# Attention with rotary embedding and two MoE layers: the first two head pairs scored on 128 rows, fillers moved, last activations of attention reordered

## The chip, the cores and the metric

The kernel runs on one core of a Trainium2 chip. The metric is the device time of one execution in microseconds, median of the runs; before the change it is 603.07 us (three runs, 602.18 to 604.75). The engines are named as in the profile: PE (TensorE, matmuls; PEld is its weight load), DVE (VectorE), ACT (ScalarE), POOL (GpSimd), SP (the queue that issues the DMAs).

## The reference

```python
q_rot, k_rot = rotate(q), rotate(k)            # rotary embedding, (2, 8, 576, 64) each
scores = matmul(q_rot, k_rot^T) / sqrt(64)
attn = softmax(scores)                         # max, exp, sum, divide
x = (attn @ v) -> (1152 tokens, 512)
h = x @ w1_in;  x = elu(h) @ w1_out            # 512 -> 2048 -> 512
h = x @ w2_in;  out = (h * tanh(softplus(h))) @ w2_out
```

The inputs of attention are float32; the weights come as float64 and are converted on the way (DVE and POOL, L96 to L108). To keep float32 accuracy on PE, the kernel splits each operand into a high part (rounded to the fast matmul type) and a low remainder, and adds up the products high by high, low by high and high by low.

## The kernel before

**Pairs and units.** Two heads of 64 dimensions share the 128 partitions: eight head pairs p. A pair has nine units of scores (`tiles`): four blocks of 128 queries for head 0, four for head 1 (L358 gives their order), and a ninth unit that holds the last 64 queries of both heads. Unit u is scored by `do_S`, u = 9p + i. The main loop (L581) takes two units per step w: step w scores units 2w and 2w+1, takes their maxima on DVE (`do_max`, L403) and exponentials on ACT (`do_exp`, L416), and transposes the probabilities P of the two units of step w-1 on PE (`do_T`, L463); the first transpose is copied out by DVE (L479), the second by ACT (L481). There is one PSUM tile for transposes, so the second waits for the first one's copy. `do_av` (L487) multiplies by v a few chunks per step, `do_R` brings the inverse sums into the same layout, `do_x`, `do_xh`, `do_xl` scale the result and split it into XH and XL. A score tile has two PSUM buffers, so a unit is scored when the exponential of the unit two before it is done. Each engine works off its instructions in the order written.

**Two ways of scoring.** For pairs 2 to 7 (`DIRECT`, L376) DMAs stack the parts on 128 partitions ("ka" holds the high part of k over its low part, "qa" twice the high part of q, "qb" the low part over zeros), and a block takes two passes of 128 rows. For pairs 0 and 1 there is no time for this: a block takes three passes on the 64 partitions of its head, `d["qh"][rows, cols]` against `d["kh"][rows, ks]` and so on. The ninth unit uses 128 rows in every pair ("bh", "bl", filled by four small DMAs in `stack_q`).

**Who prepares what.** `rope_part` rotates in three operations, on DVE for k of pair 0, else on POOL. Pair 0 is split piecewise as its data land (`HEAD`, `first_hi` on ACT, `first_lo` on DVE). From pair 1 on, `prepare(p, k)` is called at set places: k=0 splits k (`split_half`: high and low part on POOL, for pair 1 the high part on ACT) and k=1 splits q (both on POOL), each with its DMAs; k=2 to 7 rotate pair p+1 on POOL. The tile "qh" of pairs 1 to 7 has one buffer: POOL can write it for pair 2 only when PE has scored the last block of pair 1.

**Fillers.** `keep_warm(n)` puts n matmuls of zeros by zeros on PE (each shows as two instructions, L533): 20 at the start, and `FILL = (0, 9, 0)`: none after the scores of step 0, nine after those of step 1.

**End of attention.** The first three products of the first MoE layer (`g1_mm`, L207, n = 0, 1, 2) are placed in steps 36, 37 and 38 (`tail(k, False)`). Their activation `elu` is three ACT operations and two on DVE, the second of which (L242) frees the score tile; `elu_hi` on ACT and `elu_lo` on DVE split the result. `tail(k, True)` does this for product 0 at the end of step 37, behind `do_xh` and `do_x` of that step, and for product 1 at the end of step 38. Product n needs the PSUM buffer of product n-2.

The functions that the change touches, with the profile's line numbers:

Of the kernel before, what the change touches and what calls it, by code (L numbers as in the profile page):

```python
# [22 lines left out]
def plain(ap):  # L23
    return ap.bitcast(F32)
# [3 lines left out]
def kernel(  # L28
# [25 lines left out]
    TPP = 9  # L54
# [199 lines left out]
    def attention(att, ps, tail):  # L254
# [3 lines left out]
        psA = [ps.tile([128, 512], F32, name=f"psA{g}") for g in range(2)]  # L258
        HEAD = [(2, slice(0, HS)), (0, slice(0, 128)), (2, slice(HS, S)), (0, slice(128, HS)), (0, slice(HS, S))]
        WARM = 20  # L260
        FILL = (0, 9, 0)
        DIRECT = 2 * TPP
        QSCALE = -1.0 / float(D) ** 0.5
        qk_t = {}
        v_t = {}
# [35 lines left out]

        def split_alloc(p):
            d = {}
            for nm in ("kh", "kl", "ql"):
                d[nm] = att.tile([128, S], F32R, tag=nm, name=nm, bufs=2)
            for nm in (("qa",), (), ("ka", "qa"))[min(p, 2)]:
                d[nm] = att.tile([128, 2, S], F32R, tag=nm, name=nm, bufs=2)
            d["qh"] = att.tile([128, S], F32R, tag="qh", name="qh", bufs=1) if p else d["qa"][:, 0, :]
            i = p % 2
            d["qb"] = qb[i]  # L310
            d["bh"], d["bl"] = bd[i]
            sp_t[p] = d

        def split_half(p, i, h, l):
            d = sp_t[p]
# [4 lines left out]
                nc.gpsimd.tensor_scalar(out=d[h], in0=x, scalar1=1.0, scalar2=0.0, op0=ALU.mult, op1=ALU.add)  # L320
            nc.gpsimd.tensor_tensor(out=d[l], in0=x, in1=plain(d[h]), op=ALU.subtract)

        def first_hi(i, cs):
            nc.scalar.activation(
                out=sp_t[0]["kh" if i else "qh"][:, cs], in_=qk_t[0][:, i, cs],
                func=AF.Copy, scale=1.0 if i else QSCALE,
            )

        def first_lo(i, cs):
            d = sp_t[0]  # L330
            h, l = ("kh", "kl") if i else ("qh", "ql")
            nc.vector.scalar_tensor_tensor(
                out=d[l][:, cs], in0=qk_t[0][:, i, cs], scalar=1.0 if i else QSCALE,
                in1=plain(d[h][:, cs]), op0=ALU.mult, op1=ALU.subtract,
            )

        def spread(dst, src, r):
            for h in range(2):
                nc.sync.dma_start(out=plain(dst[64 * r:64 * r + 64, h, :]), in_=plain(src[64 * h:64 * h + 64, :]))

        def stack_k(p):
            d = sp_t[p]
            if p > 1:
                spread(d["ka"], d["kh"], 0)
                spread(d["ka"], d["kl"], 1)

        def stack_q(p):
            d = sp_t[p]
            for r in range(2 if p > 1 else 0):
                spread(d["qa"], d["qh"], r)  # L350
            if p > 1:
                spread(d["qb"], d["ql"], 0)
            for r in range(2):
                sl = slice(64 * r, 64 * r + 64)
                nc.sync.dma_start(out=plain(d["bh"][sl, 64 * r:64 * r + 64]), in_=plain(d["qh"][sl, S - 64:S]))
                nc.sync.dma_start(out=plain(d["bl"][sl, 64 * r:64 * r + 64]), in_=plain(d["ql"][sl, S - 64:S]))

        tiles = [(0, 0), (0, 1), (1, 0), (1, 1), (0, 2), (0, 3), (1, 2), (1, 3), None]  # L358
        psS = {}
# [7 lines left out]
        def do_S(u):  # L367
            p, i = divmod(u, TPP)
            d = sp_t[p]
            o = ps_s()  # L370
            psS[u] = o
            if tiles[i] is not None:
                h, t = tiles[i]
                rows = slice(64 * h, 64 * h + 64)
                cols = slice(128 * t, 128 * t + 128)
                if u >= DIRECT:  # L376
                    passes = [
                        (d["qa"][:, h, cols], lambda ks: d["ka"][:, h, ks]),
                        (d["qb"][:, h, cols], lambda ks: d["ka"][:, h, ks]),
                    ]  # L380
                else:
                    passes = [
                        (d["qh"][rows, cols], lambda ks: d["kh"][rows, ks]),
                        (d["ql"][rows, cols], lambda ks: d["kh"][rows, ks]),
                        (d["qh"][rows, cols], lambda ks: d["kl"][rows, ks]),
                    ]
            else:
                passes = [
                    (d["bh"], lambda ks: d["kh"][:, ks]),
                    (d["bh"], lambda ks: d["kl"][:, ks]),  # L390
                    (d["bl"], lambda ks: d["kh"][:, ks]),
                ]
            n = len(passes)
            for a, (l, r) in enumerate(passes):
                for j in range(2):
                    nc.tensor.matmul(  # L396
                        o[:, j, :HS], lhsT=l, rhs=r(slice(j * HS, j * HS + HS)),
                        start=(a == 0), stop=(a == n - 1),
                    )

        def do_max(u):
            m = att.tile([128, 1], F32, tag="mn", name="mn", bufs=4)
# [122 lines left out]
            bd.append(pair)  # L525
        qb = [att.tile([128, 2, S], F32R, name=f"qb{i}") for i in range(2)]
        nc.vector.memset(psT[:, 1, 0:128], 0.0)
        for t in qb:
            nc.vector.memset(plain(t[64:128]), 0.0)
        split_alloc(0)  # L530
        def keep_warm(n):
            for _ in range(n):
                nc.tensor.matmul(psA[1][:, 0:128], lhsT=zero, rhs=zero, start=True, stop=True)  # L533
# [3 lines left out]
        for i, cs in HEAD:  # L537
            rope_half(0, i, nc.vector if i else nc.gpsimd, cs)
            if cs.stop < S or i:
                first_hi(i, cs)  # L540
        for i, cs in HEAD[:-1]:
            first_lo(i, cs)
        nc.scalar.activation(out=tab[:, 0:2, :], in_=tab[:, 2:4, :], func=AF.Copy, scale=QSCALE)
        rope_half(1, 2, nc.gpsimd)

        def prepare(p, k):
            if k == 0:
                if p > 1 and p + 1 < NP:
                    load_pair(p + 1)
                split_alloc(p)  # L550
                split_half(p, 2, "kh", "kl")
                stack_k(p)
            elif k == 1:
                split_half(p, 0, "qh", "ql")
                stack_q(p)
            elif p + 1 < NP:
                rope_part(p + 1, 2 if k < 5 else 0, (k - 2) % 3, nc.gpsimd)
# [23 lines left out]
        for w in range(max(av_at) + 2):  # L581
# [36 lines left out]
                do_T(b - 2)  # L618
            if R is not None:
                do_R(*R)  # L620
            if last_end is not None:
                do_xh(*last_end)
                if w > max(av_at):
                    do_xl(*last_end)
# [5 lines left out]
                load_pair(2)  # L630
            if 0 < w <= NW:
                do_evac(b - 2, nc.scalar)
            if w in (1, 2):
                if w == 2:
                    rope_half(1, 0, nc.gpsimd)
                prepare(1, w - 1)
            elif w in (3, 4):
                for k in range(3):
                    prepare(1, 3 * w - 7 + k)
            if end is not None:  # L640
                do_x(*end)
            if w >= NW:
                tmp_pool[0] = att
                tail(w - NW, True)
                tmp_pool[0] = None
            weight_slot(w, (1, 2, 3, 4))
        assert not R_t
        assert njob[0] == len(STAGES) and not staged
# [188 lines left out]

    def tail(k, late):
        if late:
            if k in (1, 2):  # L840
                elu_lo(*elu_hi(*elu(0, k - 1, 0, early[k - 1])))
                early[k - 1] = None
        elif k < 3:
            early[k] = g1_mm(0, k, 0)

# [62 lines left out]
```

## Time and profile before

| | |
|---|---|
| median of three runs | 603.07 us |
| profiled execution | 608.24 us, of which the span is 606.5 us |
| mean granted clock of PE over the span | 0.971 |
| PE busy | 572.2 us (94%) |
| DVE busy | 426.3 us (70%) |
| ACT busy | 360.3 us (59%) |
| POOL busy | 240.7 us (40%) |
| mean of a maximum (DVE L403), of an exponential (ACT L416) | 0.752 us, 0.737 us |
| releasers of PE's idle time from 0 to 62 us | DVE's copy of transposes 3.1 us, DVE's memset of bl 1.5 us, ACT's kh 1.3 us, the DMA of qa 1.0 us |

The granted clock is a share of full speed: 1.00 is 2.4 GHz, 0.50 is 1.2 GHz. "Busy" on PE does not mean full speed: at 0.50 the same matmul takes up to twice as long and counts as busy all along. Attention fills the span up to about 184 us, the first MoE layer to about 412 us, the second the rest. In the page's 40 slices PE is at 9 tenths or more in every slice from the fourteenth (197 us) on, but for the 28th (409 to 425 us) and the last.

### The profile page before, as it was taken

Reading aid. Unit: us, or ns where it says so; the run is one execution under the profiler, and the core shown is the slowest. Engines: PE = TensorE matmul, PEld = TensorE weight load, DVE = VectorE, ACT = ScalarE, POOL = GpSimd, SP = SyncE. Lnnn points to the kernel's source line nnn. Section 1 sums busy time; section 2 is a strip of 40 time slices with the busy share of each in tenths; the row PEclk is TensorE's granted clock in tenths of the full one; section 3 lists DMA queues with packets and bytes.
Section 4 is the critical chain, followed back from the end, with each engine's and each line's share of the span. In section 5 each row is a group of like instructions: output and inputs, shape, how many; then the busy total and the mean of one; then the engine's idle time right before and its main releaser. Section 6 shows DMA issues by size and latency. Waiting matters only on the chain.

```text
span 606.5 us, 10180 instructions
## 1 busy us (share of the span) xinstructions
PE 572.2 (94%) x3850; PEld 511.4 (84%) x3850; DVE 426.3 (70%) x642; ACT 360.3 (59%) x642; POOL 240.7 (40%) x212
## 2 busy tenths in 40 slices
PE   7899989988996999999999999996999999999997
PEld 6766667666785999999999999995799898999985
DVE  6366888988844776677777777898488677674552
ACT  3446657666664656555455465783866858478660
POOL 5483989972021132323323222445244433432000
PEclk8689999999998999999999999999799999999999
DMA  6263786856011122323223223233242432300022
GB/s 216 71 204 102 205 224 204 225 129 159 24 47 35 47 94 78 97 70 98 77 74 102 69 70 105 71 113 112 71 110 76 128 88 73 118 19 1 17 88 86
DMA packets 43121, 60.69 MB, mean 100 GB/s; under 512 B 13760, under 2 KB 31936, under 8 KB 42304
## 3 DMA queue, kind: packets, MB, share of 16 engines
q1 hardware_dynamic: 43072, 60.05, 33.1%
q8 instruction: 30, 0.49, 0.3%
q14 instruction: 19, 0.16, 0.1%
HBM read 46.20 MB, written 2.36 MB: 80 GB/s over the span
## 4 chain that ended last, share of the span: by engine, by line
PE 39%; issue 32%; DVE 13%; POOL 13%; DMA 1%; SPq 1%; ACT 1%; POOLq 0%; DVEq 0%; ACTq 0%
PE ps_h L742 17%; PE ps_s L207 13%; PE ps_s L396 4%; POOL wu L96 4%; DVE mn L403 4%; PE psT L463 4%; DVE pt L479 3%; POOL wi1l L128 3%; POOL wo0l L128 2%; POOL wo1l L128 2%; POOL wi0l L128 2%; PE psA L487 1%; DVE wu L104 1%; DVE R L432 1%; DVE wu L108 1%
## 5 line engine op out<-in xcount | busy, mean ns | idle before, releaser
L416 ACT ACTIVATE P<-ps_s,mn 128x576 f32<-128x576 f32 x72 | 52.8, 737 | 34.3 <-DVE mn L403 34.0
L403 DVE TENSOR_REDUCE mn<-ps_s 128x1 f32<-128x576 f32 x72 | 51.9, 752 | 29.1 <-PE ps_s L396 29.0
L463 PE MATMUL psT<-idn,P 128*128 128x128 f32 (+1 forms) x360 | 55.6, 287 | 12.9 <-DVE pt L479 12.8
L463 PEld LDWEIGHTS psT<-idn,P 128*128 128x128 f32 (+1 forms) x360 | 39.4, 139 | 31.1 <-DVE pt L479 25.8
L207 PE MATMUL ps_s<-XH,wi0h 128*128 128x288 f32 x256 | 55.7, 300 | 5.5 <-DVE P L242 5.4
L128 POOL TENSOR_TENSOR wo0l<-wu,wo0h 128x512 fp32r<-128x512 f32 x16 | 25.3, 1582 | 87.3 <-ACT wo0h L125 87.3
L100 DVE TENSOR_SCALAR wu<-wu 128x512 int32<-128x512 int32 x64 | 34.2, 534 | 35.1 <-POOL wu L96 35.1
L207 PE MATMUL ps_s<-XH,wi1h 128*128 128x288 f32 x256 | 55.1, 296 | 1.4 <-ACT tb L670 1.4
L128 POOL TENSOR_TENSOR wi1l<-wu,wi1h 128x512 fp32r<-128x512 f32 x16 | 25.3, 1578 | 78.2 <-ACT wi1h L125 78.2
L207 PE MATMUL ps_s<-XL,wi0h 128*128 128x288 f32 x256 | 55.2, 297 | 0.0
L207 PE MATMUL ps_s<-XH,wi0l 128*128 128x288 f32 x256 | 55.1, 297 | 0.0
L207 PE MATMUL ps_s<-XH,wi1l 128*128 128x288 f32 x256 | 54.8, 295 | 0.0
L207 PE MATMUL ps_s<-XL,wi1h 128*128 128x288 f32 x256 | 54.8, 295 | 0.0
L104 DVE SCALAR_TENSOR_TENSOR wu<-raw,wu 128x512 int32<-128x512 int32 x64 | 50.1, 782 | 1.8
L108 DVE SCALAR_TENSOR_TENSOR wu<-raw,wu 128x512 int32<-128x512 int32 x64 | 48.9, 765 | 1.6
L128 POOL TENSOR_TENSOR wo1l<-wu,wo1h 128x512 fp32r<-128x512 f32 x16 | 24.0, 1503 | 63.4 <-ACT wo1h L125 63.4
L96 POOL TENSOR_SCALAR wu<-raw 128x512 f32<-128x512 f32 x64 | 46.3, 724 | 7.2 <-DMA raw<-in_w_in_dram 2.0
L207 PEld LDWEIGHTS ps_s<-XH,wi0h 128*128 128x128 f32 x256 | 42.2, 192 | 7.3 <-issue 6.2
L487 PE MATMUL psA<-pt,v_t 128*64 128x256 f32 (+1 forms) x320 | 47.4, 423 | 0.0
L241 DVE SCALAR_TENSOR_TENSOR tb<-ta,tb 128x576 f32<-128x576 f32 x30 | 22.7, 758 | 34.1 <-ACT tb L240 33.9
L238 ACT ACTIVATE tb<-ps_s 128x576 f32<-128x576 f32 x30 | 19.5, 651 | 43.4 <-PE ps_s L207 43.4
L481 ACT ACTIVATE pt<-psT 128x640 f32<-128x640 f32 x36 | 25.4, 706 | 33.1 <-PE psT L463 33.1
(148 smaller groups left out, 1540.0 us busy)
## 6 DMA issues: line engine op xcount, KB each, us to landing
raw<-in_w_in_dram SPq DMA_DIRECT2D x32, 512.0 KB, 3.7
raw<-in_w_out_dram SPq DMA_DIRECT2D x32, 512.0 KB, 3.3
qk_t<-in_qk_dram SPq DMA_DIRECT2D x6, 1152.0 KB, 7.2
qa<-qh SPq DMA_DIRECT2D x24, 144.0 KB, 2.5
v_t<-in_vp_dram SPq DMA_DIRECT2D x8, 320.0 KB, 3.6
out_dram<-Y SPq DMA_DIRECT2D x9, 256.0 KB, 2.0
ka<-kh SPq DMA_DIRECT2D x12, 144.0 KB, 3.7
ka<-kl SPq DMA_DIRECT2D x12, 144.0 KB, 3.4
```

The lines of the kernel that those rows point to most:

```text
L96: nc.gpsimd.tensor_scalar(out=u, in0=high.bitcast(F32), scalar1=REBASE, scalar2=0.0, op0=ALU.mult, op1=ALU.add)
L100: nc.vector.tensor_scalar(out=ui, in0=ui, scalar1=3, scalar2=0x7FFFFFF8, op0=ALU.logical_shift_left, op1=ALU.bitwise_and)
L104: nc.vector.scalar_tensor_tensor(out=ui, in0=high, scalar=-0x80000000, in1=ui, op0=ALU.bitwise_and, op1=ALU.bitwise_or)
L108: nc.vector.scalar_tensor_tensor(out=ui, in0=low, scalar=29, in1=ui, op0=ALU.logical_shift_right, op1=ALU.bitwise_or)
L128: nc.gpsimd.tensor_tensor(out=lo, in0=u, in1=plain(hi), op=ALU.subtract)
L207: nc.tensor.matmul(o[:, j, :HS], lhsT=w[:, cc, :], rhs=x[:, b, cc, j * HS:j * HS + HS], start=(k == 0), stop=(k == 3 * NC - 1),)
L403: nc.vector.tensor_reduce(out=m, in_=psS[u][:, :, :HS], axis=AX.XY, op=ALU.min)
L416: nc.scalar.activation(out=P.rearrange("p (j n) -> p j n", j=2), in_=psS.pop(u)[:, :, :HS], func=AF.Exp, scale=-1.0, bias=mn_t.pop(u), acc ...
L463: nc.tensor.transpose(tv[:w, c, :], P[:, c * 128:c * 128 + w], idn)
L481: eng.activation(out=o, in_=t, func=AF.Copy)
L487: nc.tensor.matmul(o[64 * h:64 * h + 64, :n], lhsT=v_t[p][:, c, 64 * h:64 * h + 64], rhs=pt_t[p, g][:, h, c, :], start=(c == 0), stop=(c = ...
L742: nc.tensor.matmul(o, lhsT=l, rhs=w, start=(k == 0), stop=(k == 3 * GF - 1))
```

## The change

Pairs 0 and 1 (`MASKED = 2`) are no longer scored on the 64 partitions of a head. "qa" and "qb" become tiles with a plane for each head, in which the other head's 64 partitions are zero; a pass multiplies such a plane by the whole of "kh" or "kl", 128 rows. The number of passes (three) stays. "own" names a head's partitions in its plane; `first_lo` (cut below) does on DVE for "qb" and "kl" what `first_hi` does on ACT, and the small DMAs of `stack_q` read from these planes. In `keep_warm(FIRST.get((a, j), 0))` a is the pass and j the half of the columns.

```diff
-        FILL = (0, 9, 0)
-        DIRECT = 2 * TPP
+        FIRST = {(0, 0): 6, (0, 1): 2}
+        FILL = (4, 5, 0)
+        MASKED = 2
...
-            for nm in ("kh", "kl", "ql"):
+            for nm in ("kh", "kl") if p < MASKED else ("kh", "kl", "ql"):
                 d[nm] = att.tile([128, S], F32R, tag=nm, name=nm, bufs=2)
-            for nm in (("qa",), (), ("ka", "qa"))[min(p, 2)]:
+            for nm in ("qa",) if p < MASKED else ("ka", "qa"):
                 d[nm] = att.tile([128, 2, S], F32R, tag=nm, name=nm, bufs=2)
-            d["qh"] = att.tile([128, S], F32R, tag="qh", name="qh", bufs=1) if p else d["qa"][:, 0, :]
+            if p >= MASKED:
+                d["qh"] = att.tile([128, S], F32R, tag="qh", name="qh", bufs=1)
...
+            if p < MASKED:
+
+                eng = nc.gpsimd if p else nc.vector
+                for nm in ("qa", "qb"):
+                    for h in range(2):
+                        eng.memset(plain(d[nm][64 - 64 * h:128 - 64 * h, h, :]), 0.0)
...
+        def own(t, h, cs):
+            return t[64 * h:64 * h + 64, h, cs]
+
+        def first_hi(i, cs, heads=(0, 1)):
+            x = qk_t[0][:, i, cs]
+            if i:
+                nc.scalar.activation(out=sp_t[0]["kh"][:, cs], in_=x, func=AF.Copy)
+            for h in () if i else heads:
+                nc.scalar.activation(
+                    out=own(sp_t[0]["qa"], h, cs), in_=x[64 * h:64 * h + 64], func=AF.Copy, scale=QSCALE,
+                )
...
+            for h in () if i else heads:
+                nc.vector.scalar_tensor_tensor(
+                    out=own(d["qb"], h, cs), in0=x[64 * h:64 * h + 64], scalar=QSCALE,
+                    in1=plain(own(d["qa"], h, cs)), op0=ALU.mult, op1=ALU.subtract,
+                )
+
+        def second_q():
+            d = sp_t[1]
+            x = qk_t[1][:, 0, :]
+            al = slice(0, S)
+            for h in range(2):
+                xh = x[64 * h:64 * h + 64]
+                nc.scalar.activation(out=own(d["qa"], h, al), in_=xh, func=AF.Copy)
+                nc.vector.tensor_tensor(
+                    out=own(d["qb"], h, al), in0=xh, in1=plain(own(d["qa"], h, al)), op=ALU.subtract
+                )
...
-                        (d["qh"][rows, cols], lambda ks: d["kh"][rows, ks]),
-                        (d["ql"][rows, cols], lambda ks: d["kh"][rows, ks]),
-                        (d["qh"][rows, cols], lambda ks: d["kl"][rows, ks]),
+                        (d["qa"][:, h, cols], lambda ks: d["kh"][:, ks]),
+                        (d["qb"][:, h, cols], lambda ks: d["kh"][:, ks]),
+                        (d["qa"][:, h, cols], lambda ks: d["kl"][:, ks]),
                     ]
...
+                    if u == 0:
+                        keep_warm(FIRST.get((a, j), 0))
...
-        for t in qb:
-            nc.vector.memset(plain(t[64:128]), 0.0)
         split_alloc(0)
+        split_alloc(1)
...
-                first_hi(i, cs)
+                first_hi(i, cs, (0,))
         for i, cs in HEAD[:-1]:
-            first_lo(i, cs)
+            first_lo(i, cs, (0,))
+        first_hi(0, slice(0, HS), (1,))
+        first_lo(0, slice(0, HS), (1,))
...
-                split_alloc(p)
+                if p > 1:
+                    split_alloc(p)
...
-                split_half(p, 0, "qh", "ql")
+                if p < MASKED:
+                    second_q()
+                else:
+                    split_half(p, 0, "qh", "ql")
                 stack_q(p)
...
+            if w >= NW:
+                tmp_pool[0] = att
+                tail(w - NW, True)
+                tmp_pool[0] = None
             if last_end is not None:
                 do_xh(*last_end)
...
-            if w in (1, 2):
-                if w == 2:
-                    rope_half(1, 0, nc.gpsimd)
-                prepare(1, w - 1)
-            elif w in (3, 4):
-                for k in range(3):
-                    prepare(1, 3 * w - 7 + k)
+            if w == 1:
+                prepare(1, 0)
+                rope_half(1, 0, nc.gpsimd)
+            elif w == 3:
+                prepare(1, 1)
+                for k in range(2, 8):
+                    prepare(1, k)
+            elif w in (5, 9):
+
+                nc.vector.memset(plain(qb[w // 9][64:128, 1, :]), 0.0)
             if end is not None:
                 do_x(*end)
-            if w >= NW:
-                tmp_pool[0] = att
-                tail(w - NW, True)
-                tmp_pool[0] = None
...
-            if k in (1, 2):
-                elu_lo(*elu_hi(*elu(0, k - 1, 0, early[k - 1])))
-                early[k - 1] = None
+            if k < 2:
+                elu_lo(*elu_hi(*elu(0, k, 0, early[k])))
+                early[k] = None
```

So the activation of product 0 moves from the end of step 37 into step 36, that of product 1 from step 38 into step 37, each ahead of that step's second copy (L481), `do_xh` and `do_x`.

## Rows read from the trace of the kernel before

**Rows 1.** Windows: start:end, length, busy (count) by engine, PE clock, DMA share, GB/s.

```profile
8.00:12.00 4.00, 1.99 (x8) 1.14 (x8) 3.97 (x7) 1.83 (x3) 3.88 (x5) 1.00 1.00 381
12.00:22.30 10.30, 9.88 (x40) 8.71 (x39) 3.10 (x5) 3.86 (x10) 4.93 (x4) 0.50 0.03 11
22.30:25.70 3.40, 2.51 (x18) 2.15 (x18) 2.30 (x5) 1.27 (x2) 0.36 (x1) 1.00 0.04 10
25.70:36.00 10.30, 9.31 (x39) 6.70 (x38) 3.95 (x6) 4.28 (x10) 9.99 (x8) 0.50 0.39 124
36.00:60.36 24.36, 22.14 (x166) 15.72 (x165) 17.04 (x27) 14.03 (x34) 12.79 (x11) 1.00 0.57 177
```

**Rows 2.** Windows, the middle of the second MoE layer's start.

```profile
400.00:500.00 100.00, 93.65 (x559) 84.36 (x558) 74.24 (x105) 68.29 (x108) 42.63 (x35) 0.95 0.33 99
```

**Rows 3.** Timeline, head: start, us, engine, line, op, out<-in, count [idle before <-releaser].

```profile
11.25 0.92 DVE L332 SCALAR_TENSOR_TENSOR ql<-qk_t,qa 128x160 fp32r<-128x160 f32 x1
...
17.00 4.21 PE L533 MATMUL psA<-bl 128*128 128x128 f32 x18
...
22.31 0.82 DVE L479 COPY pt<-psT 128x640 f32<-128x640 f32 x1 [4.45 <-PE psT L463]
23.05 0.45 DVE L332 SCALAR_TENSOR_TENSOR ql<-qk_t,qa 128x288 fp32r<-128x288 f32 x1
...
23.88 0.52 PE L396 MATMUL ps_s<-kh,qa 64*128 64x288 f32 x2
...
29.65 0.84 PE L396 MATMUL ps_s<-kh,qa 64*128 64x288 f32 x2
...
36.51 0.51 PE L396 MATMUL ps_s<-kh,bh 128*128 128x288 f32 x2
```

**Rows 4.** Timeline, transposes followed by scores, on 64 and on 128 rows.

```profile
40.22 0.77 PE L463 MATMUL psT<-idn,P 128*128 128x128 f32 x5
40.92 0.53 PE L396 MATMUL ps_s<-kh,qh 64*128 64x288 f32 x2
...
97.76 0.77 PE L463 MATMUL psT<-idn,P 128*128 128x128 f32 x5
98.28 0.51 PE L396 MATMUL ps_s<-ka,qa 128*128 128x288 f32 x2
```

**Rows 5.** Timeline, the start of pair 2.

```profile
41.31 1.44 DVE L438 TENSOR_SCALAR R<-rc 128x128 f32<-128x128 f32 x1
...
55.84 0.67 POOL L320 TENSOR_SCALAR qh<-qk_t 128x576 fp32r<-128x576 f32 x1 [9.03 <-issue]
...
60.39 0.50 PE L396 MATMUL ps_s<-ka,qa 128*128 128x288 f32 x2 [1.02 <-DMA qa<-qh]
...
61.53 0.53 PE L396 MATMUL ps_s<-ka,qb 128*128 128x288 f32 x2 [0.64 <-DMA qb<-ql]
```

**Rows 6.** Timeline, the end of attention.

```profile
175.40 0.43 PE L207 MATMUL ps_s<-XH,wi0l 128*128 128x288 f32 x2
...
178.16 0.71 ACT L481 ACTIVATE pt<-psT 128x640 f32<-128x640 f32 x1 [4.27 <-PE psT L463]
...
179.75 0.65 ACT L238 ACTIVATE P<-ps_s 128x576 f32<-128x576 f32 x1
...
181.57 2.91 PE L487 MATMUL psA<-pt,v_t 128*64 128x320 f32 x20
...
185.79 0.75 DVE L242 TENSOR_TENSOR P<-P,ps_s 128x576 f32<-128x576 f32 x1
186.57 0.68 ACT L247 ACTIVATE ge<-P 128x576 fp32r<-128x576 f32 x1 [4.75 <-DVE P L242]
...
186.69 0.50 PE L207 MATMUL ps_s<-XH,wi0h 128*128 128x288 f32 x2 [2.21 <-DVE P L242]
...
193.34 0.82 PE L207 MATMUL ps_s<-XH,wi0h 128*128 128x288 f32 x2 [3.22 <-DVE P L242]
...
197.70 0.42 PE L207 MATMUL ps_s<-XH,wi0l 128*128 128x288 f32 x2
```

More of the change, by code (lines that the diff above doesn't have):

```diff
@@ L321, in split_half, with first_lo @@
             nc.gpsimd.tensor_tensor(out=d[l], in0=x, in1=plain(d[h]), op=ALU.subtract)
[L323 to L329, printed above, removed]
-            d = sp_t[0]
[L331 to L335, printed above, removed]
+        def own(t, h, cs):
[8 more added lines that the diff above has]
+                )
+        def first_lo(i, cs, heads=(0, 1)):
+            d = sp_t[0]
+            x = qk_t[0][:, i, cs]
+            if i:
+                nc.vector.tensor_tensor(out=d["kl"][:, cs], in0=x, in1=plain(d["kh"][:, cs]), op=ALU.subtract)
+            for h in () if i else heads:
[13 more added lines that the diff above has]
+                )
         def spread(dst, src, r):
@@ L342, in stack_k @@
             d = sp_t[p]
-            if p > 1:
+            if p >= MASKED:
                 spread(d["ka"], d["kh"], 0)
@@ L348, in stack_q @@
             d = sp_t[p]
-            for r in range(2 if p > 1 else 0):
-                spread(d["qa"], d["qh"], r)
-            if p > 1:
+            if p >= MASKED:
+                for r in range(2):
+                    spread(d["qa"], d["qh"], r)
                 spread(d["qb"], d["ql"], 0)
@@ L354, in stack_q @@
                 sl = slice(64 * r, 64 * r + 64)
-                nc.sync.dma_start(out=plain(d["bh"][sl, 64 * r:64 * r + 64]), in_=plain(d["qh"][sl, S - 64:S]))
-                nc.sync.dma_start(out=plain(d["bl"][sl, 64 * r:64 * r + 64]), in_=plain(d["ql"][sl, S - 64:S]))
+                ec = slice(S - 64, S)
+                hi, lo = (own(d[nm], r, ec) for nm in ("qa", "qb")) if p < MASKED else (d["qh"][sl, ec], d["ql"][sl, ec])
+                nc.sync.dma_start(out=plain(d["bh"][sl, 64 * r:64 * r + 64]), in_=plain(hi))
+                nc.sync.dma_start(out=plain(d["bl"][sl, 64 * r:64 * r + 64]), in_=plain(lo))
         tiles = [(0, 0), (0, 1), (1, 0), (1, 1), (0, 2), (0, 3), (1, 2), (1, 3), None]
@@ L373, in do_S @@
                 h, t = tiles[i]
-                rows = slice(64 * h, 64 * h + 64)
                 cols = slice(128 * t, 128 * t + 128)
-                if u >= DIRECT:
+                if p >= MASKED:
                     passes = [
```

## The prediction

> **What bounds the kernel now.** I read the windows first, for the granted clock by stage, then the timeline of PE in the same stretch, then who releases PE at the places where it stops.
>
> The windows show two stretches at 0.50 (1.2 GHz), 10.30 us each, from 12.00 to 22.30 and from 25.70 to 36.00 us [rows 1]. In both PE is busy nearly all along (9.88 and 9.31 of 10.30 us): it is the bound, at half speed. From 36 us on the level is 1.00, though PE is busy for a smaller share (22.14 of 24.36 us). What differs is the work. Ahead of the first fall PE had 1.99 us of work in 4.00. Ahead of the rise at 22.3 us stand fillers and transposes [rows 3], ahead of the stretch that stays low the scores on 64 rows. So here scoring on 64 rows did not bring the upper level back, and fillers, though they multiply zeros, did.
>
> The timeline gives the price. Steps 2 and 3 begin at 23.88 and 29.65 us and step 4 at 36.51 [rows 3]: 5.77 and 6.86 us. Steps 4 to 8 run at 1.00 and last 60.39 - 36.51 = 23.88 us; less 1.02 and 0.64 us of waits for the DMAs of pair 2 [rows 5] that is 4.44 us a step.
>
> Those two waits come from POOL: it starts the high part of q of pair 2 only at 55.84 us, after 9.03 us idle [rows 5], because "qh" has one buffer and pair 1 was being scored from it.
>
> At the end of attention PE stops twice for DVE's L242, 2.21 us before 186.69 and 3.22 us before 193.34 [rows 6]: the score tiles are free only when the activations of products 0 and 1 are through. Product 0 is ready at about 175.7, but its first ACT operation starts at 179.75, behind the copy at 178.16 and what follows it, and DVE's half stands behind `do_x`, which waits for the 2.91 us of attention times v that start at 181.57.
>
> **The change part by part.**
>
> *Head, to step 2.* DVE gets one more low part (head 1, 288 columns) ahead of the first maximum. The same number of columns took 0.45 us alone, while 160 columns beside POOL's work took 0.92, ending at 12.17 [rows 3]. Bounds 0.45 and 1.9; I take 0.9, nearest to the second row, since POOL rotates at that time as well. Maximum 0 then starts at about 13.1. With 0.75 for a maximum and 0.74 for an exponential (the page's means, in the table above), exponentials 0 and 1 end at 14.6 and 15.5; the units of step 1 wait for these buffers and are scored by 16.4 (0.8 us a unit at the upper level). Eighteen filler instructions took 4.21 us at 0.50 [rows 3], so I estimate half of that, 0.12 us, at 1.00: five fillers are 1.2 us (to 17.6). The 6 + 2 in unit 0 and the 4 behind unit 1 stand in gaps where PE would wait (2.0 of 4.00 us idle, [rows 1]); at 0.50 they would cost up to 1.9 us beyond the gaps. Then transposes 0.77 [rows 4], DVE's copy 0.82 [rows 3], transposes 0.77: step 2 starts at 20.0 in place of 23.88. The added ACT pieces (two of 64 rows for one of 128) fall into ACT's gaps, the memsets at the start (four on DVE for two of twice the length, four on POOL) ahead of the first data; without that cover they cost up to 2 us.
>
> *Steps 2 and 3 at 1.00.* 4.44 us each, less a gain in the switches: the scores follow the transposes by 40.92 - 40.22 = 0.70 us on 64 rows and by 98.28 - 97.76 = 0.52 on 128 [rows 4]. I take 0.18 a step (bounds 0 and 0.3). Step 4 then starts at 20.0 + 2 x 4.26 = 28.5, for 36.51: **8.0 us** gained. If the clock falls once as it did before, steps of 5.77 and 6.86 come back and 4 of these are lost.
>
> *Steps 4 to 8.* `second_q` puts two ACT operations and two DVE operations between step 3 and the maxima of step 4. Behind them wait the exponentials on ACT, the maxima on DVE, and through these PE. One DVE operation takes about 0.75 us (L242 has the same length, [rows 6]), up to 1.0 more beside POOL. Bounds 0 (if PE has other work) and 3.5; I take 1.6, the two at 0.75 with a little of ACT. Against it: 5 x 0.18 = 0.9 for the switches, and the two DMA waits, 1.66, since POOL no longer waits for "qh" of pair 1; next late there is the load of pair 3, which nothing in this stretch needs. But POOL then works in the 9 us in which it idled, and a DVE operation beside it can be held: 1.44 us for a [128, 128] multiply in [rows 5]. I take one such hold, 1.0 (bounds 0 and 2). The memsets in steps 5 and 9 stand where DVE waits for scores; uncovered, 0.5 each. Sum: 1.66 + 0.9 - 1.6 - 1.0 = **0.0**.
>
> *End of attention.* Product 0 ends at 175.7. Its three ACT operations (0.65 to 0.7 each, as L238 and L247 in [rows 6]) run to 177.8, DVE's two to 179.4, `elu_hi` to 180.1. The copy that stood at 178.16 now ends at 180.8, the copies of R at 181.5: just where attention times v starts (181.57), with PE filled by product 1 until then; no cover is left, a microsecond more on ACT delays PE by one. Product 2 follows attention times v at once, at 184.5, since its buffer has been free since 179.4; product 3 at 187.7. Product 1 (done 181.5) frees its buffer at 185.3. Product 4 needs that of product 2: on ACT its activation waits behind `elu_hi` of product 1, both `do_xh` and a weight copy, to 189.3; plus 2.1 on ACT and 1.6 on DVE, product 4 starts at 193.0. Before it started at 197.96 (0.26 us after the row at 197.70). **5.0 us** gained; bounds 3.0 (ACT 2 us later) and 7.1 (product 4 straight behind product 3). From there on PE is busy without a gap in the page's slices, so the gain stays.
>
> *Sum.* 8.0 + 0.0 + 5.0 = 13.0 us, made against the profiled execution: 606.5 us of span and 1.74 around it, 608.24. This is 5.17 us above the median; it has a stretch at 0.50 in the second layer (mean 0.95 from 400 to 500 us, [rows 2]), which lies outside the change, and I take it that the median lacks it. The head is taken to be the same in both. 603.07 - 13.0 = **590.0 us**.
>
> *A rule weighed.* In [rows 1] PE is busy for 9.31 of 10.30 us and the level stays at 0.50. The Trainium skill, "TensorE: Matmul & The Clock Gate", section "The HAM clock gate (the 'warmup' mystery)", says that the gate is set by how busy PE has been of late; it says nothing of rows. The trace disagrees as far as it goes, and the fourth rival below is what that rule would do.
>
> **The rivals.** Measurements of this kernel tell about 0.5% (3 us) from no change.
>
> 1. *As summed*, 0.55: 590.0, own range 586 to 593.5.
> 2. *One fall in the head or in step 4*, 0.20, where `second_q` leaves PE with some 2.8 us of work in 4.4. For it: the fall at 12 us came after a half idle stretch [rows 1]. Against: the level held from 36 us on through steps with waits. Price 4: 594.
> 3. *The end gives little*, 0.12: ACT, now full from 175.7 to 181.5, delays attention times v, or product 4 waits longer. Against: each piece has its row. 2 of the 5 us are lost, or all: 592 to 595, I take 594.
> 4. *Rows make no difference to the clock*, 0.08, so the change does not do what it says: falls at 12 and 25.7 as before, step 4 at 36.5 + 0.9 for the added low part. Gain 5.0 - 0.9 + 0.0: 599.
> 5. *The other side*, 0.05: zeros in half the rows count for less than 64 full rows, and with the nine fillers cut to five PE does not get back to 1.00 until pair 2. Place: steps 4 to 8. A step at 0.50 took 6.86 us against 4.44 [rows 3], so each costs 2.4. The gain at the end (5.0) is used up from the third such step on; with five, and 4 us of head in which there was a warm stretch and fillers were fewer, 603.07 + 12 + 4 - 5.0 + 0.9 = 615. Against: fillers of zeros did raise the level.
>
> **How the numbers follow.** The forecast is the first case. Low end 585.5: the first case with second_q and the hold at their lower bounds and 2 us more at the end. High end 598: it holds the second and third cases and leaves out the last two (0.13) and some of the tails. Faster by over 0.5% (under 600.05): cases 1 to 3 and most of the fourth, 0.89 after a little for what I have not seen; within 0.5%: 0.06; slower 0.05.
>
> **What would show it.** Clock 1.00 from about 6 us to 40 us; step 2 at about 20 and step 4 at about 28.5 us; POOL's "qh" of pair 2 before 45 us and no PE wait for its DMAs; step 9 about 8 us earlier than 60.4; at the end no PE wait on L242 before product 2 and one of about 2 us before product 4, 13 us earlier than 197.96. Wrong would be: a level of 0.50 between 12 and 40 us, PE waiting for "qb" of pair 1 by more than 2 us, or attention times v starting later after product 1 than before.

## The result, and the profile after

The changed kernel takes 595.57 us (median of four runs, 595.13 to 596.55), the kernel before 603.35 beside it (602.18 to 604.75): ratio 0.9872 [0.9847, 0.9898], 7.8 us faster where 13.0 were forecast. Its profiled execution took 596.55 us (span 594.8, mean granted clock 0.991). The profiled execution of before took 608.24 at 0.971, so the two traces lie 11.7 us apart and the medians 7.8. The profiled execution of before is one of its slower and colder ones, as the experiments show.

Windows of the kernel after, columns as in [rows 1] (the engines in the order PE, PEld, DVE, ACT, POOL), the last line being the start of the second MoE layer:

```profile
8.00:12.00 4.00, 3.99 (x35) 3.77 (x34) 3.94 (x8) 2.02 (x4) 3.75 (x5) 1.00 0.96 381
12.00:22.30 10.30, 7.84 (x61) 7.12 (x60) 7.67 (x13) 6.88 (x17) 6.73 (x6) 1.00 0.05 11
22.30:25.70 3.40, 2.95 (x24) 2.86 (x24) 1.48 (x3) 1.85 (x5) 3.32 (x4) 1.00 1.00 342
25.70:36.00 10.30, 7.53 (x55) 5.56 (x54) 7.66 (x9) 5.61 (x13) 10.14 (x8) 1.00 0.27 90
36.00:60.36 24.36, 22.14 (x171) 17.07 (x171) 19.88 (x33) 14.37 (x35) 17.79 (x16) 1.00 0.77 230
...
400.00:440.00 40.00, 33.63 (x183) 29.00 (x182) 27.94 (x37) 25.13 (x41) 18.30 (x16) 0.87 0.34 102
```

The level is 1.00 in all five windows of the head; in [rows 1] it is 0.50 in two of them. PE is no longer the engine that is full: 7.53 of 10.30 us from 25.7 us on, with POOL at 10.14. In the second layer a stretch below 1.00 stands in this trace too (0.87 over 40 us).

Timeline of the head, kernel after, columns as in [rows 3]; the last line, from the first MoE layer, is for comparison with L361:

```profile
19.34 0.51 PE L425 MATMUL ps_s<-kh,qa 128*128 128x288 f32 x2
23.49 0.51 PE L425 MATMUL ps_s<-kh,qa 128*128 128x288 f32 x2
25.37 0.74 ACT L447 ACTIVATE P<-ps_s,mn 128x576 f32<-128x576 f32 x1 [0.83 <-DVE mn L434]
26.91 0.76 PE L494 MATMUL psT<-idn,P 128*128 128x128 f32 x5
27.43 0.51 PE L425 MATMUL ps_s<-kh,bh 128*128 128x288 f32 x2
28.32 1.38 ACT L360 ACTIVATE qa<-qk_t 64x576 fp32r<-64x576 f32 x2
29.02 2.84 DVE L361 TENSOR_TENSOR qb<-qk_t,qa 64x576 fp32r<-64x576 f32 x2 [2.16 <-ACT qa L360]
29.43 1.81 POOL L297 TENSOR_TENSOR qk_t<-qk_t 128x576 f32<-128x576 f32 x1
30.02 0.53 PE L425 MATMUL ps_s<-kh,qb 128*128 128x288 f32 x2 [0.45 <-DVE qb L361]
31.21 1.91 POOL L293 TENSOR_TENSOR qk_t<-qk_t,tab 128x576 f32<-128x576 f32 x1
31.89 1.42 DVE L434 TENSOR_REDUCE mn<-ps_s 128x1 f32<-128x576 f32 x2
32.74 0.74 ACT L447 ACTIVATE P<-ps_s,mn 128x576 f32<-128x576 f32 x1 [3.05 <-DVE mn L434]
34.65 1.49 DVE L463 TENSOR_SCALAR R<-rc 128x256 f32<-128x256 f32 x1
44.23 0.71 POOL L96 TENSOR_SCALAR wu<-raw 128x512 f32<-128x512 f32 x1 [6.08 <-DMA raw<-in_w_in_dram]
44.92 0.66 POOL L328 TENSOR_SCALAR qh<-qk_t 128x576 fp32r<-128x576 f32 x1
52.86 0.51 PE L425 MATMUL ps_s<-ka,qa 128*128 128x288 f32 x2
...
348.04 0.76 DVE L767 TENSOR_TENSOR XL<-Y,XH 128x576 fp32r<-128x576 f32 x1 [0.75 <-ACT XH L766]
```

Steps 2, 3, 4 and 9 start at 19.34, 23.49, 27.43 and 52.86 us, for 23.88, 29.65, 36.51 [rows 3] and 60.39 [rows 5]. The wait for the DMA of "qa" at step 9 is gone, and "qh" of pair 2 is written at 44.92 in place of 55.84. DVE's two low parts at L361 take 2.84 us, and the next exponential on ACT waits 3.05 us for a maximum behind them.

The end of attention, kernel after, to compare with [rows 6]; the rows are the starts of product 0's last pass, its activation, the copy for attention times v, products 2 and 4:

```profile
168.71 0.43 PE L207 MATMUL ps_s<-XH,wi0l 128*128 128x288 f32 x2
169.17 0.65 ACT L238 ACTIVATE P<-ps_s 128x576 f32<-128x576 f32 x1 [1.97 <-PE ps_s L207]
173.46 0.69 ACT L512 ACTIVATE pt<-psT 128x640 f32<-128x640 f32 x1
174.87 2.91 PE L518 MATMUL psA<-pt,v_t 128*64 128x320 f32 x20
177.71 0.53 PE L207 MATMUL ps_s<-XH,wi0h 128*128 128x288 f32 x2
186.05 0.54 PE L207 MATMUL ps_s<-XH,wi0h 128*128 128x288 f32 x2 [1.70 <-DVE tb L242]
```

The activation follows its product by 0.46 us; before, 4.35 us (179.75 - 175.40). Attention times v starts 6.70 us earlier, as much as product 0 itself, so it isn't delayed; product 2 has no wait, and product 4 one of 1.70 us.

Trace against trace, the 11.7 us come about so: step 4 earlier by 9.08; 1.55 given back in steps 4 to 8; 0.83 between step 9 and product 0 (165.69 for 172.39, 6.70 earlier); 5.21 more by product 4 (186.05 for 197.96, 11.91 earlier), of which 0.2 are given back behind it.

### The profile page after: what moved, and what is told of

It reads as the page before. It is cut to its first block, busy times and chain, and to the rows that moved or that the text cites. A ratio compares the mean times of both kernels' runs of the same rounds, so it can differ in the third digit from the quotient of the medians.

```text
span 594.8 us, 10228 instructions
## 1 busy us (share of the span) xinstructions
PE 562.9 (95%) x3866; PEld 506.9 (85%) x3866; DVE 430.5 (72%) x650; ACT 362.5 (61%) x646; POOL 242.5 (41%) x214
## 4 chain that ended last, share of the span: by engine, by line
PE 38%; issue 30%; DVE 16%; POOL 13%; ACT 2%; DMA 1%; SPq 0%; POOLq 0%; DVEq 0%; ACTq 0%
PE ps_h L781 17%; PE ps_s L207 13%; DVE mn L434 4%; POOL wu L96 4%; PE ps_s L425 3%; DVE pt L510 3%; PE psT L494 3%; POOL wi1l L128 3%; POOL wo0l L128 2%; POOL wo1l L128 2%; POOL wi0l L128 2%; DVE R L463 2%; DVE wu L104 2%; DVE wu L108 1%; ACT P L447 1%
## 5 line engine op out<-in xcount | busy, mean ns | idle before, releaser
L494 PE MATMUL psT<-idn,P 128*128 128x128 f32 (+1 forms) x360 | 53.0, 278 | 16.4 <-DVE pt L510 16.2
L494 PEld LDWEIGHTS psT<-idn,P 128*128 128x128 f32 (+1 forms) x360 | 38.2, 134 | 32.9 <-DVE pt L510 30.0
L100 DVE TENSOR_SCALAR wu<-wu 128x512 int32<-128x512 int32 x64 | 32.8, 513 | 35.2 <-POOL wu L96 35.2
L207 PE MATMUL ps_s<-XH,wi1h 128*128 128x288 f32 x256 | 55.1, 296 | 1.4 <-ACT tb L709 1.4
L96 POOL TENSOR_SCALAR wu<-raw 128x512 f32<-128x512 f32 x64 | 46.8, 732 | 11.3 <-DMA raw<-in_w_in_dram 6.1
L708 ACT ACTIVATE ta<-ps_s 128x576 f32<-128x576 f32 x32 | 20.6, 644 | 40.2 <-PE ps_s L207 40.2
```

The source lines that it names most:

```text
L96: nc.gpsimd.tensor_scalar(out=u, in0=high.bitcast(F32), scalar1=REBASE, scalar2=0.0, op0=ALU.mult, op1=ALU.add)
L100: nc.vector.tensor_scalar(out=ui, in0=ui, scalar1=3, scalar2=0x7FFFFFF8, op0=ALU.logical_shift_left, op1=ALU.bitwise_and)
L207: nc.tensor.matmul(o[:, j, :HS], lhsT=w[:, cc, :], rhs=x[:, b, cc, j * HS:j * HS + HS], start=(k == 0), stop=(k == 3 * NC - 1),)
L494: nc.tensor.transpose(tv[:w, c, :], P[:, c * 128:c * 128 + w], idn)
```

## Experiments

The gain of 7.8 us for 13.0 has to be explained. Theory A: the terms hold, but the head of the profiled execution of before was colder than in most executions, so in medians the head gives less. Rivals: B, the median of before lacks the second-layer stretch, and the terms are wrong; C, the end gives less than 5 us in medians. "Before in the same job" is the kernel before, run between the others on the same chip.

**1. The kernel before once more, unchanged.**

> The kernel before, unchanged, profiled and timed once more. The profiled executions of before and after differ by 11.7 us (608.24 and 596.55), the medians by 7.8. Theory A (the head of the recorded profile was colder than usual): this profile shows a shorter time at 0.50 ahead of 36 us than the 20.6 us recorded, step 4 starting at 32 to 34 us and not at 36.5, the stretch at 0.50 in the second layer present, time 602 to 605. Rival B (what the prediction assumed: the median lacks the stretch at 0.50 in the second layer): the head looks as recorded, step 4 at 36 to 37 us, but the level is 1.00 all along from 400 to 500 us. Rival C (the spell at 0.50 at the end of attention, 192.97 to 196.38, is what comes and goes): head and second layer as recorded, no spell at 193 us.

Twelve runs, median 604.37 us, 600.49 to 609.59. Its profile (609.12 us, clock 0.977) has both stretches at 0.50 in the head, so that step 4 starts about as late as in [rows 3], and the stretch in the second layer:

```profile
36.98 0.51 PE L396 MATMUL ps_s<-kh,bh 128*128 128x288 f32 x2
```

What A wanted of this trace didn't come, and B's didn't either. The last case of the expectation (no spell at 0.50 at 193 us, all else as recorded) is what the trace shows, with a level of 1.00 from 160 to 200 us. But at 609.12 us this execution is no faster than the first profiled one, so that spell is not what parts the profile from the median. What speaks for A is the spread: 46 executions of before in two jobs took 600.3 to 610.1 us at mean clocks of 0.989 to 0.971, and twelve were above 608, as both of these profiled ones are; ten of the changed kernel took 595.06 to 597.04 at 0.991 to 0.994. From the mean clock I estimate the time at 0.50 (twice what the mean lacks to 1.00, times the span): 35 us in the first profiled execution (0.971), 24 us at the median mean clock of the 46 (0.980), 7 to 11 us in the changed kernel. The median execution of before thus lacks about as much as one stretch of 10.3 us.

**2. The end alone, on the kernel before.**

```diff
+            if w >= NW:
+                tmp_pool[0] = att
+                tail(w - NW, True)
+                tmp_pool[0] = None
             if last_end is not None:
...
-            if k in (1, 2):
-                elu_lo(*elu_hi(*elu(0, k - 1, 0, early[k - 1])))
+            if k < 2:
+                elu_lo(*elu_hi(*elu(0, k, 0, early[k])))
```

> The kernel before with only the new order at the end of attention (activation of products 0 and 1 one step earlier, ahead of do_xh and do_x). Theory: product 4 starts 5.0 us earlier after attention times v than before, all of it kept: 5 us faster than before, about 598. Rival (part of it is given back in the first layer, which waits for weights): 2 to 3 us faster, about 600.5, with a wait of PE on weights between 190 and 412 us.

598.43 us (597.56 to 603.46, six runs) for 605.01, 0.9897 [0.9844, 0.995]. C falls: from the start of product 0 to that of product 4 it takes 189.01 - 168.66 = 20.35 us, after 20.36, before 25.57. Its head, with the instructions of before, shows what A needs. Windows, then timeline of PE, kernel with the end alone:

```profile
8.00:12.00 4.00, 1.27 (x4) 0.90 (x4) 3.65 (x7) 1.50 (x3) 3.18 (x5) 0.90 0.92 371
12.00:22.30 10.30, 10.07 (x43) 8.94 (x42) 3.82 (x6) 4.21 (x11) 5.62 (x5) 0.54 0.01 4
25.70:36.00 10.30, 9.31 (x68) 6.96 (x67) 6.25 (x9) 6.45 (x15) 10.05 (x8) 1.00 0.35 124
...
400.00:440.00 40.00, 33.64 (x197) 29.59 (x196) 29.02 (x40) 24.97 (x41) 18.65 (x15) 0.91 0.29 92
```

```profile
23.89 0.53 PE L396 MATMUL ps_s<-kh,qa 64*128 64x288 f32 x2
28.35 0.53 PE L396 MATMUL ps_s<-kh,qa 64*128 64x288 f32 x2
32.41 0.51 PE L396 MATMUL ps_s<-kh,bh 128*128 128x288 f32 x2
...
168.66 0.51 PE L207 MATMUL ps_s<-XH,wi0h 128*128 128x288 f32 x2
...
189.01 0.54 PE L207 MATMUL ps_s<-XH,wi0h 128*128 128x288 f32 x2 [1.69 <-DVE tb L242]
```

Step 2 starts as in [rows 3], but the second stretch at 0.50 is missing: from 25.7 us on the level is 1.00, at the same busy 9.31 of 10.30 us (in which PE gets through 68 instructions and not 39). Step 4 starts at 32.41, 4.10 us earlier than in [rows 3]; at product 0 it is 3.73. Measured from this execution the head of the changed kernel gives 6.70 - 3.73 = 2.97 us, and with the end 5.2 that makes 8.2: close to the 7.8 of the medians. No profile of the kernel before itself in such an execution is on record; this head stands in for it.

**3. The changed kernel and its head alone (the new end taken back), in one job.** The edit is that of experiment 2 the other way round, on the changed kernel.

> The changed kernel once more, on the chip of the three below. Theory (its head keeps the upper level in every execution, and one stretch at 0.50 in the second layer stays): all executions within 3 us, 594 to 597, mean clock 0.99; the kernel before spreads over 8 us beside it. Rival (it falls in the head in some executions as well): a spread of 4 us or more, mean clocks down to 0.98.

> The changed kernel with the old order at the end of attention. Theory (the two gains add up): 5.2 us slower than the changed kernel, 600 to 601.5, PE waiting on L242 for 2.2 and 3.2 us as before. Rival (with the head faster, the weights come late and hide part of it): less than 4 us slower.

The changed kernel took 595.95 us (595.06 to 597.04), its head alone 601.1 (598.48 to 602.4, twelve runs), before 603.89 in the same job (600.32 to 609.86). So in medians the end is worth 5.15 us and the head 2.8 (0.9945 [0.9914, 0.9975]). Waits of PE from 160 to 200 us with the head alone (us in total, times, longest):

```profile
PE ps_s L207 <- DVE P L242: 3.9, 2, 2.2
...
PE ps_s L207 <- DVE tb L242: 0.9, 1, 0.9
```

The first of the old waits is as before (2.21 us), the second shorter (1.7 for 3.22); with the new end one wait of 1.7 us is left. Part of the old end's cost is clock: after the first of these waits (180.73 us) pairs of matmuls take 0.69 us in place of 0.42, up to 184 us.

**4. Rows or fillers?** The changed kernel with 64 rows, without fillers, and without both.

```diff
-                        (d["qa"][:, h, cols], lambda ks: d["kh"][:, ks]),
+                        (d["qa"][rows, h, cols], lambda ks: d["kh"][rows, ks]),
...
-        FIRST = {(0, 0): 6, (0, 1): 2}
-        FILL = (4, 5, 0)
+        FIRST = {}
+        FILL = (0, 0, 0)
```

(In the first part the other two passes likewise, with `rows` the 64 partitions of head h.)

> The changed kernel, but a block of pairs 0 and 1 is multiplied on the 64 partitions of its head again, from the same tiles; fillers, second_q, memsets and the order at the end stay changed. Theory (rows count for the clock): the level falls to 0.50 in the head once more and steps 2 and 3 take 5 us or more each; 3 to 8 us slower than the changed kernel, 599 to 604. Rival (the fillers and the filled gaps keep the clock, rows make no difference): level 1.00 throughout the head, and only the switches between 64 and 128 rows come back, 0.18 us a step: within 1.5 us of the changed kernel, 595.5 to 597.

> The changed kernel without any of its fillers in the head behind the first 20 (FIRST empty, FILL = (0, 0, 0)). Theory (128 rows alone keep the level): level 1.00 from 6 us on, step 2 starts 1 us earlier than at 19.3 since five fillers no longer stand ahead of the transposes: 0 to 1 us faster than the changed kernel, about 595. Rival (the fillers hold the level, the rows only what follows): the level falls to 0.50 between 10 and 16 us, steps 1 and 2 take 1.5 to 2.4 us more each, 2 to 5 us slower, 598 to 601.

> The changed kernel with both taken away: blocks of pairs 0 and 1 on 64 rows, and no fillers behind the first 20. With 64 rows and fillers one run fell to 0.50 from 24 us on (median 598.5); with 128 rows and no fillers one fell from 10.8 to 17.6 us (596.3). Theory (each of the two keeps the level in its own part: fillers and filled gaps up to 20 us, 128 rows behind it): falls in both parts, 600 to 606, two stretches at 0.50 ahead of 40 us. Rival (one of them is enough, or the level is a matter of chance): like the better of the two, 596 to 598.5.

| | with fillers | without |
|---|---|---|
| 128 rows | 595.95 (0.9872 [0.9838, 0.9905]) | 596.33 (0.9843 [0.9793, 0.9893]) |
| 64 rows | 598.49 (0.9902 [0.9864, 0.994]) | 604.13 (0.9994 [0.9963, 1.0025]) |

Each ratio is to before in its own job (128 rows with fillers and 64 without in one, the other two in another). Without fillers 128 rows are worth 7.8 us (9 by the ratios), far outside the intervals. With fillers the difference is 2.5 us (2 by the ratios) and the intervals overlap: the time lies between theory and rival. On 128 rows the fillers make no difference that these runs can tell. The kernel with neither is as slow as before in spite of the new end, so its head is some 5 us slower than that of before, which had nine fillers and no `second_q`: the 7.8 us are not what the change as a whole gains by its rows. For that compare within one job: with 64 rows and all the rest of the change 598.49, with the new end alone (experiment 2) 598.43. So the gain of the head goes with the rows, as far as these runs can tell. Windows of the kernel without fillers, of that with 64 rows, and of that with neither:

```profile
12.00:22.30 10.30, 8.07 (x43) 7.22 (x43) 7.15 (x12) 6.40 (x15) 6.21 (x6) 0.70 0.07 20
22.30:25.70 3.40, 2.37 (x20) 2.32 (x20) 1.53 (x3) 2.14 (x6) 3.40 (x3) 1.00 0.82 298
```

```profile
12.00:22.30 10.30, 8.90 (x64) 7.51 (x62) 7.29 (x12) 6.50 (x15) 6.54 (x6) 1.00 0.06 15
22.30:25.70 3.40, 2.41 (x11) 2.02 (x11) 0.95 (x2) 1.98 (x6) 3.32 (x4) 0.68 0.92 328
25.70:36.00 10.30, 8.81 (x38) 6.47 (x36) 4.43 (x5) 3.61 (x7) 10.14 (x8) 0.61 0.02 8
```

```profile
12.00:22.30 10.30, 7.55 (x31) 6.20 (x31) 5.65 (x10) 6.08 (x14) 5.24 (x5) 0.52 0.03 9
22.30:25.70 3.40, 3.10 (x13) 2.37 (x12) 1.71 (x3) 1.56 (x4) 3.35 (x3) 0.50 0.77 262
25.70:36.00 10.30, 9.61 (x39) 7.41 (x40) 2.97 (x4) 2.97 (x9) 9.92 (x8) 0.50 0.07 31
```

With 128 rows and no fillers the level falls for 6.8 us (from about 11.3) and comes back. With fillers and 64 rows it holds past the last filler (17.6 us) and falls from about 23.5 to 33.7 us and from 37.2 to 40.6; that execution is a cold one, for six of the twelve had mean clocks of 0.990 to 0.993, like the changed kernel, and took 596.61 to 598.65 us. With neither it stays down for 23.9 us, with PE busy for 9.61 of 10.30, and all twelve executions are as cold (0.965 to 0.974).

The fourteen traces of this case sort by the two parts. In the five without fillers in step 0 PE works for 1.27 to 2.57 of the 4.00 us from 8 to 12 us, and the level falls between 11.1 and 12.4 us; in the nine with them it works for 2.88 to 4.00 us, and the level holds. From 22 to 40 us the level is at 0.50 for a time in four of the five traces with 64 rows (experiment 2 is the exception) and in none of the nine with 128.

**5. The cost of `second_q`: split over steps 3 and 4, ahead of ACT's copy.**

```diff
+            if w in (3, 4):
+                second_q(w - 3)
             if 0 < w <= NW:
                 do_evac(b - 2, nc.scalar)
+            if w == 4:
+                stack_q(1)
...
             elif w == 3:
-                prepare(1, 1)
```

> The changed kernel with second_q cut in two: head 0 of q of pair 1 in step 3, ahead of ACT's copy there (where ACT waits), head 1 with its four DMAs in step 4. In the changed kernel the exponentials of steps 3 and 4 are 7.37 us apart, against 4.10 in the run of the kernel before with the new end, whose head is at the upper level there. Theory (second_q stands between the scores of step 4 and their maxima, 3.3 us): the distance falls to 4.5 to 5, and 2 to 3 us are kept to the end: 592.5 to 593.5. Rival (DVE is held by POOL's rotation of pair 2 whatever the place): the low parts take 1.4 us each again and hold up step 5 in place of step 4: under 1 us, 594.5 to 596.

594.91 us (594.35 to 595.84), 0.9854 [0.9817, 0.989]: 1.0 us less than the changed kernel in the same job, which the intervals do not tell apart. The stop moved and did not go: the first exponentials of steps 3 and 4 stand 4.0 us apart (25.37 to 32.74 = 7.4 after), those of steps 4 and 5 then 6.26. The low parts, in this kernel's timeline:

```profile
28.16 1.01 DVE L361 TENSOR_TENSOR qb<-qk_t,qa 64x576 fp32r<-64x576 f32 x1 [0.74 <-ACT qa L360]
...
32.56 1.38 DVE L361 TENSOR_TENSOR qb<-qk_t,qa 64x576 fp32r<-64x576 f32 x1 [1.02 <-ACT qa L360]
```

**6. The low parts on POOL; then one filler group fewer.**

```diff
-                nc.vector.tensor_tensor(
+                nc.gpsimd.tensor_tensor(
...
+            if w == 3:
+                prepare(1, 1)
             if 0 < w <= NW:
                 do_evac(b - 2, nc.scalar)
```

The second kernel has `FILL = (4, 0, 0)` besides.

> The changed kernel with second_q ahead of ACT's copy in step 3 and both its low parts on POOL, ahead of the rotation of pair 2, in place of DVE. Cutting second_q in two moved the delay from step 4 to step 5 and gave 1.0 us. Theory (what costs is a low part on DVE beside POOL, 1.0 to 1.4 us each and then behind it the maxima; POOL's rotation has slack, 6 us idle before 44.2 in the changed kernel's trace): the exponentials of steps 3 and 4 come 4.3 to 5 us apart, those of 4 and 5 under 5, 2 to 3 us are kept: 593 to 594. Rival (POOL has no slack: pair 2 comes late): the gain is back to under 1 us at step 9, PE waits there for qa or qb: 595 to 596.

> The same as the kernel with second_q's low parts on POOL, and without the five fillers of step 1, which stand ahead of the transposes there (1.2 us on the way to step 2). Theory (128 rows and the fillers of step 0 are enough for the level): step 2 starts 1 us earlier, mean clock 0.99 still, 0.5 to 1 us faster than with the five, about 592.5. Rival (the five are needed in some executions): mean clocks of 0.985 to 0.988 in part of the executions and a median equal or up to 2 us slower.

594.93 us (593.25 to 596.85), 0.9866 [0.983, 0.9902], and 595.29 (592.92 to 596.58), 0.9865 [0.9826, 0.9904]: not told apart from the changed kernel, nor from each other. In the trace of the first the exponentials of steps 3 and 4 are 4.0 us apart, and step 8 comes 2.2 us earlier; step 9 gives it back:

```profile
43.39 1.74 SPq L78 DMA_DIRECT2D raw<-in_w_in_dram  x3
47.65 0.66 POOL L96 TENSOR_SCALAR wu<-raw 128x512 f32<-128x512 f32 x1 [5.44 <-DMA raw<-in_w_in_dram]
48.27 0.67 POOL L328 TENSOR_SCALAR qh<-qk_t 128x576 fp32r<-128x576 f32 x1
52.83 0.51 PE L425 MATMUL ps_s<-ka,qa 128*128 128x288 f32 x2 [1.92 <-DMA qa<-qh]
```

POOL waits 5.44 us for weights, "qh" stands behind it, and step 9 starts at 52.83, as it does after (52.86). The weights come late because of POOL itself: their load stands in SP's queue behind the DMAs of k of pair 2, and POOL, which now does the low parts first, gets to the low part of that k at 40.80 for 36.76 us (L329); the load is issued at 43.39 for 39.35, 4.0 us later, of which 0.8 us is a later head in this execution (step 4 at 28.27 for 27.43). Behind step 9 the level falls to 0.50 for 3.4 us (55.1 to 58.5), and step 10 starts at 58.92, later than after (57.51).

**7. That conversion one step later (with and without the filler group).**

```diff
     STAGES = [
-        (5, 8, 9, 10, 11, 13), ...
+        (6, 8, 9, 10, 11, 13), ...
```

> The kernel with second_q's low parts on POOL, and the first weight conversion (wu, L96) one step later, in step 6 and not 5. In the run with the low parts on POOL steps 4 to 8 were 2.2 us ahead of the changed kernel, and all of it was lost at step 9, where PE waited 1.92 us for qa and 0.61 for qb of pair 2: on POOL the high part of q of pair 2 stood behind L96, which waited 5.4 us for its weights to land. Theory: with L96 behind it the high part is written before 44 us, PE waits less than 0.3 us for pair 2 at step 9, exponential 18 comes at 52.5 to 53.5, and 2 us more than before are kept: 592.5 to 593.5. Rival (the loss comes back elsewhere, on DVE beside a POOL that then works without a break): step 9 is ahead by 2 us, step 20 by less than 0.5: 594.5 to 595.5.

> The same without the five fillers of step 1. In the pair of runs before this the exponentials of step 2 came at 20.97 without them and at 22.04 with them, and the lead was 0.9 us still at the end of attention, while the medians (595.3 and 594.9) did not tell them apart. Theory (a lead of 0.9 us is kept): 0.9 us faster than with the five, 591.5 to 592.5. Rival (it is lost in executions that fall to 0.50 somewhere): no difference within 0.5 us.

600.55 us (599.0 to 601.35), 0.9944 [0.9915, 0.9973], and 600.05, 0.9942 [0.9913, 0.9971]: some 5 us slower than without the move, against what I expected. Timeline of the first:

```profile
49.00 1.69 SPq L78 DMA_DIRECT2D raw<-in_w_in_dram  x3
53.25 0.64 POOL L96 TENSOR_SCALAR wu<-raw 128x512 f32<-128x512 f32 x1 [8.29 <-DMA raw<-in_w_in_dram]
53.92 1.61 DVE L100 TENSOR_SCALAR wu<-wu 128x512 int32<-128x512 int32 x1 [4.97 <-POOL wu L96]
60.39 1.33 PE L494 MATMUL psT<-idn,P 128*128 128x128 f32 x5 [7.65 <-DVE pt L510]
```

Step 9 now starts at 49.87, without a wait, as wanted. But the stage number moves the load with the conversion: its DMAs are issued at 49.00, behind those of `stack_q(2)`, and no longer at 43.39 (experiment 6). POOL waits 8.29 us for them, DVE's next conversion 4.97 for POOL, the copy of the transposes stands behind that and what follows it on DVE, and PE waits 7.65 us; the level is 0.50 for 10.2 us (from 55.9).

## Why the prediction was right or wrong

**The base of the sum: wrong, and most of the miss.** The step that failed is "I take it that the median lacks it" with "The head is taken to be the same in both". It is the other way round: the second-layer stretch stands in the profile of every kernel here, the changed one's (0.87) and that with the end alone (0.91) among them, while the head of before differs from execution to execution. The profiled one had two stretches at 0.50, that of experiment 2 one, and this is worth 4.1 us at step 4; the mean clocks (experiment 1) say that the median execution lacks about one such stretch. By that the 13.0 us, made against the profile, should have been some 9 against the median.

**Head: the mechanism was right, the size against the profile 9.1 for 8.0.** Step 2 came at 19.34 (20.0 foreseen), step 4 at 27.43 (28.5), scores 0.52 us behind the transposes as worked out. Against the median of before it was worth, with steps 4 to 8, 2.8 us. The reading behind the mechanism went too far in two places. "What differs is the work" does not hold: the row at 40.92 in [rows 4] is a score on 64 rows in the stretch at 1.00, and pair 1 is scored so up to 55 us. And that fillers raise the level is not shown: ahead of the rise at 22.3 us stood transposes too, and without fillers the level rose as well (experiment 4).

**Steps 4 to 8: -1.55 for 0.0.** Both DMA waits went, as foreseen. `second_q` was mis-sized: the first exponentials of steps 3 and 4 lie 7.37 us apart, 4.10 in experiment 2, so it cost 3.3 and not 1.6 (the upper bound, 3.5, held it). The two low parts took 1.42 us each beside POOL's rotation, not 0.75 (1.01 and 1.38 in experiment 5); a subtraction of as many columns, also with two operands in SBUF, took 0.74 to 0.76 us in all its eight places (L767). POOL's operations beside them took 1.81 and 1.91 us, the ones before them 1.40 to 1.41. The Trainium skill, "SBUF — State Buffer", section "Who interferes with whom", states that DVE and GpSimd share a port pair under an exclusive lock. The trace agrees in so far as both engines got longer side by side. The hold was there as well (L463, 1.49 us; 0.29 at its shortest). Experiment 6 shows that taking this cost off DVE brings 2.2 us up to step 8, and that the load of weights, and POOL behind it, sets step 9 then: "the load of pair 3, which nothing in this stretch needs" was not what is late next.

**End: right, 5.2 for 5.0** in the trace; in medians 6.6 alone (experiment 2, with a wide interval) and 5.15 taken back (experiment 3); with the one wait foreseen, 1.70 us for about 2.

**The rivals.** One fall in the head didn't come in the changed kernel. The end did not give little. That rows make no difference to the clock falls: 604.13 against 596.33 without fillers. But rows aren't the whole of it, since with the fillers 64 rows reach 598.49, and in experiment 2 the level held through scores on 64 rows. The busy share by itself doesn't sort these stretches: PE was busy for 9.31 of 10.30 us at 0.50 [rows 1] and at 1.00 (experiment 2), and for 7.53 at 1.00 after. The Trainium skill, "TensorE: Matmul & The Clock Gate", section "The HAM clock gate (the 'warmup' mystery)", states that the gate is set by how busy PE has been recently. The gap from 8 to 12 us fits that, the 64 rows do not. The other side, slower, needed steps at 0.50 in pair 1; there were none.

**Still open.** What makes the head of before fall once in some executions and twice in others; why 64 rows hold the level less well than 128 with as many passes; and whether the 2.2 us can be kept by converting later while the load stays where it was, which wasn't tried.

## What to carry to other kernels

One profiled execution is one draw: compare its time and mean clock with those of all runs before a sum is made against it, and take the gain of a warm stretch only as often as the stretch is cold. A low part on DVE beside POOL's work is to be priced at up to nearly twice its length alone (1.42 us for 0.75). A load that moves takes another place in the queue (5 us in experiment 7), and work added on POOL puts off the loads that stand behind its results (by over 3 us in experiment 6). Two remedies for one fall (here more rows and fillers) don't add: each alone got at least two thirds of what both got.

## What was not expected of the hardware

The same program, from the same place on (step 2 at 23.88 and 23.89 us) and at the same busy share (9.31 of 10.30 us on PE), ran at 0.50 in one execution and at 1.00 in another. Ahead of both stood much the same: a stretch at 0.50 with PE busy for 9.88 and 10.07 us in its window, which ended about 1 us earlier where the level then held, and 3.40 us at 1.00. Without fillers the level came back after 6.8 us with 128 rows, and after 23.9 us with 64, in one trace each; the mean clocks of all their executions (0.987 to 0.994 and 0.965 to 0.974) lie apart likewise.
